# Late attention in two parts: products with v by row halves, one output product behind the scores

## The chip, the cores and the metric

The kernel runs on one core of a Trainium2 chip. The metric is the time of one execution on the device in microseconds (us). Short names: PE is the matmul engine (TensorE), PEld its loads of stationary operands, DVE is VectorE, ACT is ScalarE, POOL is GpSimd, SP the engine that issues most DMA transfers. Matmuls write into PSUM banks of 512 fp32 per partition; everything else lies in SBUF.

## The reference, cut to what matters

Attention over chunks of 32 queries (16 keys to the left, 8 to the right, and 8 memory keys: 64 keys a chunk), then a gated feed-forward on the rows of all heads:

```
for c in range(nc):                                  # 24 chunks of 32, per batch and head
    k_full = np.concatenate([mem_k, k_ctx], axis=2)  # 64 keys, some left out at the ends
    scores = scale * np.matmul(q_c, k_full.transpose(0, 1, 3, 2))
    scores = scores - np.max(scores, axis=-1, keepdims=True)
    a = np.exp(scores)
    a = a / (np.sum(a, axis=-1, keepdims=True) + 1e-09)
    out[:, :, c_start:c_end] = np.matmul(a, v_full)
...
rms = np.sqrt(np.mean(x * x, axis=-1, keepdims=True) + 1e-06)
xn = x / rms * rms_g
g = xn @ w_gate
silu = g * (1.0 / (1.0 + np.exp(-g)))
return (silu * (xn @ w_val) @ w_out)                 # 3072 x 512, w: 512 x 1536 and 1536 x 512
```

## The kernel before

**Feed-forward.** The 3072 rows are 8 blocks of 384 tokens, and the 1536 columns of the weights are 12 groups `f` of 128. For each block and `f`, `moe_in` makes the gate `pg` and the value `pv` (12 matmuls of 384 columns each), DVE and ACT make `t`, and split it into `hh` and `hl`, and `moe_out` adds 9 matmuls of 512 columns into three banks `po` (an output product). All of it runs in fp32r with operands split into a high and a low part. `moe_out` of group f-1 stands behind `pv` of group f, so that `hh` and `hl` have one group of matmuls as cover.

**Attention.** It is cut into 32 units: a batch, a half of its 768 queries, and a pair of heads. Units 0 to 7 (blocks 0 and 1) are done at the start, by an order that is written out by hand, together with the making of the split weights. The other 24 are "late": twelve pairs of units, done while the feed-forward runs. The feed-forward is then a row of seven segments: the rest of block 0 (from f = 5), and blocks 2 to 7. While one segment runs, the attention of the next block (two pairs of units) is done, and its rows are normed.

**A late visit.** `late_steps` is a generator, and one step of it is called a visit. `VISITS` says at which places of a segment the visits stand: place 2(f-f0) is behind `pg` of group f, place 2(f-f0)+1 behind `pv`. A visit has work for the pair before (`old`) and for the current pair (`cur`), in this order on PE:

- `stage_p`: six 128x128 transposes of the old pair's probabilities `pe` into two banks `pT` (the first is the bank of `pg`, tag "g");
- `stage_c`, on ACT and DVE: `pT` is copied into the buffers `pt0` and `qp1`, in four copies of 64 partitions x 384, two on each engine. The even and the odd chunk of a pair of chunks go to columns of their own, and what is left between them is zero (the buffers were set to zero once by POOL), so that one stationary operand of 128 rows holds the keys of both chunks;
- `stage_s2`: 48 score matmuls of the current pair, on tiles of 64 rows x 32 columns of the array, 64 columns each;
- `stage_m`, `stage_e` on DVE and ACT: maximum, difference, exponential;
- `stage_o`: the products with v of the old pair, 12 matmuls a unit, 128 rows x 64 columns of the array, 64 columns each, in two banks (the second is the bank of `pv`, tag "v");
- `late_r`: ACT copies each unit's result to `xT` and squares it, DVE adds the squares; after a block's second pair `late_n` makes the norm in steps ("n" in `VISITS`): two matmuls `ssum`, a polynomial for the inverse root on DVE, and at last `xT` times the norm;
- `stage_d` on DVE: sums and division of the current pair's exponentials; then the loads of q and k for the next pair and of v for the current one, on SP's queue, into single buffers.

At the end of a segment `split_x` splits `xT` into `xh` and `xl` on ACT and DVE for the next segment, with the last `hh` and `hl` between.

An fp32 matmul of these shapes stands as two instructions in the trace. The order in which PE runs what is written is fixed from the late part on (`keep_in_program_order`); on DVE, ACT and SP a scheduler places instructions by priority and estimated times, except where `issue_after` binds them.

Of the kernel before, what the change touches and what calls it, by code (L numbers as in the profile page):

```python
# [20 lines left out]
CH = 32  # L21
# [18 lines left out]
YMAX = 0x1DFE / 0x1000 * 2.0 ** -96  # L40


VISITS = (((1, "v"), (5, "v"), (9, "v"), (10, "n"), (11, "n"), (12, "n")),
# [3 lines left out]
RSQRT = (-0.49999831, 0.37499999, -0.31395044, 0.27418771)  # L47
FA, FC = 1, 5
SEQ = ([(0, f) for f in range(FA)] + [(1, f) for f in range(FA)] + [(b, f) for f in range(FA, FC) for b in range(2)]
# [21 lines left out]
def tile_kernel(ctx: ExitStack, tc: tile.TileContext, q, k, v, w_gate, w_val, w_out, rms_g, out):  # L71
# [46 lines left out]
    pts = [early.tile([P, NT, 4, 2, CH], F32, name=f"pt{i}") for i in range(2)]  # L118
    late = {}

    def zeros(t):
        nc.gpsimd.memset(t, 0.0)
        return t

    def late_buffers(i):

        if i:
            t = p1.tile([P, HT + VN], F32, name="qp1", tag="A")
            late["q", 1], late["pt", 1] = t[:, 0:HT], zeros(t[:, HT:])
            late["kv", 1] = p1.tile([P, KN + VN], F32, name="kv1", tag="B")  # L130
        else:
            late["q", 0] = p1.tile([P, HT], F32, name="q0", tag="q")
            late["pt", 0] = zeros(p1.tile([P, VN], F32, name="pt0", tag="wy"))
            late["kv", 0] = p1.tile([P, KN + VN], F32, name="kv0", tag="ws")
        late["pt", i] = late["pt", i].rearrange("p (i a s q) -> p i a s q", i=NT, a=4, s=2)

    def load_qk(u):
        d = st.setdefault(u, {})
# [16 lines left out]

    def pt_of(u):

        return pts[u % 2] if u < NE else late["pt", u % 2]

    def copy(e, out, in_):  # L160
        if e == "a":
# [68 lines left out]
    def stage_d(u):  # L230
        stage_da(u)
        stage_db(u)
# [31 lines left out]
        d["t"] = t  # L264

    def stage_c(u):
        stage_ch(u, 0, "a")
        stage_ch(u, 1, "d")

    def stage_ch(u, hh, e):  # L270
        r = slice(64 * hh, 64 * hh + 64)
        t4 = st[u]["t"][:, 0:HT].rearrange("p (i a q) -> p i a q", i=NT, q=CH)
        copy(e, pt_of(u)[r, :, :, hh, :], t4[r])

    def stage_o(u, tag=None):

        pt, vw = pt_of(u), st[u]["v"]
        o = psum_m(tag, f"o{u}") if tag else psum_a(f"o{u}")
        for j in range(NJ):
            for hh in range(2):  # L280
                on_pe(nc.tensor.matmul(o[64 * hh:64 * hh + 64, j * D:(j + 1) * D], lhsT=vw[:, j, hh],  # L281
                                 rhs=pt[:, j // 2, 2 * (j % 2) + (hh ^ (u % 2 if u >= NE else 0))].rearrange("p c q -> p (c q)"),
                                 start=True, stop=True))
        st[u]["o"] = o[:, 0:HT]

    def late_r(u, x):

        g = units[u][2]
        o = st.pop(u)["o"]
        nc.scalar.copy(x[:, g], o)  # L290
        s = obuf(f"sq{u}")[:, 0:HT]
        nc.scalar.activation(s, x[:, g], AF.Square)
        if g:
            nc.vector.tensor_tensor(out=s, in0=s, in1=late["ss"], op=ALU.add)
        late["ss"] = s

    def late_n(x):

        ss = late["ss"]
        sh, sl = [p3.tile([P, DM], F32R, name=f"s{c}", tag="stg")[:, 0:HT] for c in "hl"]  # L300
        nc.scalar.copy(sh, ss)
        nc.vector.tensor_tensor(out=sl, in0=ss, in1=sh.bitcast(F32), op=ALU.subtract)
        yield
        ps = psum_a("ssum")[:, 0:HT]
        for i, c in enumerate((sh, sl)):
            on_pe(nc.tensor.matmul(ps, lhsT=one.broadcast_to([P, P]), rhs=c, start=not i, stop=i == 1))
        s = obuf("rs")[:, 0:HT]
        nc.vector.tensor_scalar(out=s, in0=ps, scalar1=DM * 1e-6, scalar2=None, op0=ALU.add)

        r = obuf("rr")[:, 0:HT]  # L310
        nc.scalar.activation(r.bitcast(I32), s.bitcast(U32), AF.Copy, bias=float(0x5F3759DF), scale=-0.5)
        t = obuf("rt")[:, 0:HT]
        nc.vector.tensor_tensor(out=t, in0=r, in1=r, op=ALU.mult)
        nc.vector.tensor_tensor(out=t, in0=t, in1=s, op=ALU.mult)
        nc.vector.tensor_scalar(out=t, in0=t, scalar1=1.0, scalar2=None, op0=ALU.subtract)
        yield
        q = obuf("rq")[:, 0:HT]
        nc.vector.tensor_scalar(out=q, in0=t, scalar1=RSQRT[3], scalar2=RSQRT[2], op0=ALU.mult, op1=ALU.add)
        nc.vector.tensor_tensor(out=q, in0=q, in1=t, op=ALU.mult)
        for c in (RSQRT[1], RSQRT[0]):  # L320
            nc.vector.scalar_tensor_tensor(out=q, in0=q, scalar=c, in1=t, op0=ALU.add, op1=ALU.mult)
        nc.vector.scalar_tensor_tensor(out=r, in0=q, scalar=1.0, in1=r, op0=ALU.add, op1=ALU.mult)
        yield
        for kt in range(NKT):
            nc.vector.scalar_tensor_tensor(out=x[:, kt], in0=x[:, kt], scalar=rg[:, kt:kt + 1], in1=r,  # L325
                                           op0=ALU.mult, op1=ALU.mult)
        yield
# [162 lines left out]
    def obuf(name):  # L490
        return p3.tile([P, DM], F32, name=name, tag="stg")
# [64 lines left out]
    def late_steps():  # L556


        pairs = [(u, u + 1) for u in range(NE, len(units), 2)]
        for n in range(len(pairs) + 1):  # L560
            old = pairs[n - 1] if n else ()
            cur = pairs[n] if n < len(pairs) else ()
            new = pairs[n + 1] if n + 1 < len(pairs) else ()
            for u in old[0:1]:
                if u % NG == 0:
                    late_x["x"] = p1.tile([P, NKT, HT], F32, name="xT", tag="x")
            x = late_x.get("x")
            with tc.high_priority():
                for i, u in enumerate(old):
                    stage_p(u, None if i else "g")  # L570
                for u in old:
                    stage_c(u)
            if not cur:
                yield "p"
            with tc.high_priority():
                if cur:
                    stage_s2(cur)
                for u in cur:
                    stage_m(u)
                for u in cur:  # L580
                    stage_e(u)
                for i, u in enumerate(old):
                    stage_o(u, "v" if cur and i else None)
                for u in old:
                    late_r(u, x)
            norm = late_n(x) if n and n % 2 == 0 else ()
            if norm:
                with tc.high_priority():
                    next(norm)
            with tc.high_priority():  # L590
                for i, u in enumerate(cur):
                    if norm and i:
                        with tc.issue_after(last_of(nc.vector)):
                            stage_d(u)
                    else:
                        stage_d(u)
            for u in new:
                load_qk(u)
            for u in cur if n else ():
                load_v(u)  # L600
            yield "v"
            for _ in norm:
                yield "n"

# [148 lines left out]
    for sg, (blk, f0) in enumerate(segments):  # L753
        po = [psm_o(i) for i in range(NT)] if sg else sp["po", 0]
        last = sg == len(segments) - 1
        steps = {} if last else dict(VISITS[min(sg, 2) + (sg == len(segments) - 2)])

        def visit(gap):
            if gap in steps and next(todo, None) not in (steps[gap], None):
                raise AssertionError(gap)  # L760
        for f in range(f0, NF):
            g = moe_in("g", f, xs, last)
            visit(2 * (f - f0))
            out_ = lambda f=f, h=prev: moe_out(f - 1, h, po)
            if f == f0:
                out_ = lambda: None
                if sg == 0:

                    moe_out(NF - 1, prev, po1)
                    with tc.high_priority():  # L770
                        store(1, po1)
            vv = moe_in("v", f, xs, last)
            visit(2 * (f - f0) + 1)
            if f < NF - 1:
                out_()
                prev = moe_h(g, vv, blk)
            elif last:
                out_()
                finish(f, g, vv, po, blk)
            else:  # L780
                with tc.high_priority():
                    t = moe_t(g, vv, blk)
                xs = split_x(late_x["x"], t, out_, lambda h: moe_out(NF - 1, h, po))
        if sg == 0:
            behind.close()
        if not last:
            store(blk, po)
# [65 lines left out]
```

## Time and profile before

| | before |
|---|---|
| runs, median (lowest to highest) | 709.34 us (708.74 to 709.37) |
| the profiled execution, own time | 707.74 us |
| its span, first to last instruction | 705.9 us |
| mean granted TensorE clock | 0.992 |
| DVE busy | 392.3 us (56%) |
| ACT busy | 261.4 us (37%) |
| HBM read, written | 47.97 MB, 6.29 MB |

The profiled execution is one of its own beside the three timed runs; its time contains 1.84 us outside its span. In the views, a line has a start, a duration in us, the engine, the source line, the operation, what it writes and reads, shapes, and a count. A matmul's duration runs from its start until its last result, and matmuls overlap: the cost of one is read from the distance between starts.

### The profile page before, as it was taken

What the parts mean: (1) busy time and instruction counts of PE and PEld (TensorE: products, weight loads), DVE (VectorE), ACT (ScalarE), POOL (GpSimd) and SP (SyncE); (2) the same over time, 40 slices, a digit from 0 to 9 for tenths busy, and PEclk for the clock granted to TensorE, in tenths of its full rate; (3) what the DMA queues carried; (4) which work ended last, traced back from release to release, by engine and by line L of the source; (5) the groups of instructions that cost most, each with busy time, mean ns of one, the idle gap of its engine ahead of it and who ended that gap; (6) DMA issues with size and microseconds to landing.
All of it is one profiled execution on the core that took longest, in us unless ns stands there. A gap on an engine that the chain in (4) does not pass through costs nothing.

```text
span 705.9 us, 13419 instructions
## 1 busy us (share of the span) xinstructions
PE 687.4 (97%) x5702; PEld 636.3 (90%) x5702; DVE 392.3 (56%) x780; ACT 261.4 (37%) x474; POOL 6.1 (1%) x14
## 2 busy tenths in 40 slices
PE   7899999999999999999999999999999999999997
PEld 6798898999989999999999999999999999999996
DVE  6789999857674327552383525735276532552222
ACT  4697987733333113331233313222133311331112
POOL 0010000000000000000000000000000000000000
PEclk8899999999999999999999999999999999999999
DMA  9644644333321103130021303013031100010001
GB/s 319 246 167 137 235 149 139 115 132 109 115 90 51 58 0 105 46 104 1 17 90 45 105 1 89 16 46 105 1 104 46 45 3 0 1 46 1 0 1 46
DMA packets 22620, 55.14 MB, mean 78 GB/s; under 512 B 2464, under 2 KB 6816, under 8 KB 22560
## 3 DMA queue, kind: packets, MB, share of 16 engines
q1 hardware_dynamic: 19824, 49.55, 20.9%
q10 hardware_dynamic: 2736, 4.72, 1.8%
q8 instruction: 45, 0.74, 0.5%
q14 instruction: 15, 0.12, 0.1%
HBM read 47.97 MB, written 6.29 MB: 77 GB/s over the span
## 4 chain that ended last, share of the span: by engine, by line
PE 88%; DVE 5%; ACT 4%; issue 1%; DMA 1%; POOL 0%; SPq 0%; DVEq 0%; ACTq 0%
PE pg L437 27%; PE pv L437 27%; PE po L487 27%; PE o L281 3%; PE pT L263 1%; ACT pt L162 1%; DVE pt L165 1%; DVE qp L165 1%; DMA k<-in_k_dram 1%; ACT ws L392 1%; ACT ws L381 1%; PE s L184 1%; PE ss L622 1%; ACT wy L382 1%; DVE xT L325 1%
## 5 line engine op out<-in xcount | busy, mean ns | idle before, releaser
L437 PE MATMUL pv<-xh,wh_v 128*128 128x384 f32 x384 | 130.1, 339 | 2.1 <-DVE t L458 2.1
L437 PE MATMUL pg<-xh,wh_g 128*128 128x384 f32 x384 | 130.5, 340 | 0.0
L437 PE MATMUL pv<-xh,wl_v 128*128 128x384 f32 x384 | 129.7, 338 | 0.5 <-DVE wl_v L408 0.5
L437 PE MATMUL pg<-xl,wh_g 128*128 128x384 f32 x384 | 129.8, 338 | 0.0
L437 PE MATMUL pg<-xh,wl_g 128*128 128x384 f32 x384 | 129.8, 338 | 0.0
L437 PE MATMUL pv<-xl,wh_v 128*128 128x384 f32 x384 | 129.6, 337 | 0.0
L162 ACT CAST hh<-t 128x384 fp32r<-128x384 f32 x89 | 45.8, 515 | 192.7 <-PE po L487 176.0
L487 PE MATMUL po<-wh_o,hh 128*128 128x512 f32 x285 | 113.9, 400 | 0.7 <-ACT hh L744 0.6
L487 PE MATMUL po<-wh_o,hl 128*128 128x512 f32 x285 | 112.6, 395 | 0.0
L487 PE MATMUL po<-wl_o,hh 128*128 128x512 f32 x285 | 112.3, 394 | 0.0
L455 DVE SCALAR_TENSOR_TENSOR t<-t,pg 128x384 f32<-128x384 f32 x72 | 39.9, 554 | 105.8 <-ACT t L451 105.7
L467 DVE TENSOR_TENSOR hl<-t,hh 128x384 fp32r<-128x384 f32 x89 | 49.5, 556 | 85.7 <-ACT hh L162 85.6
L458 DVE TENSOR_TENSOR t<-t,pv 128x384 f32<-128x384 f32 x95 | 52.7, 554 | 71.5 <-PE pv L437 70.2
L451 ACT ACTIVATE t<-pg 128x384 f32<-128x384 f32 x72 | 35.5, 493 | 120.2 <-PE pg L437 120.2
L437 PEld LDWEIGHTS pg<-xh,wh_g 128*128 128x128 f32 x384 | 72.3, 188 | 4.1 <-DVE gr L446 0.4
L437 PEld LDWEIGHTS pg<-xl,wh_g 128*128 128x128 f32 x384 | 72.3, 188 | 3.6
L437 PEld LDWEIGHTS pv<-xh,wh_v 128*128 128x128 f32 x384 | 72.0, 188 | 3.6 <-DVE t L458 1.8
L437 PEld LDWEIGHTS pv<-xh,wl_v 128*128 128x128 f32 x384 | 72.0, 188 | 0.8 <-DVE wl_v L408 0.8
L437 PEld LDWEIGHTS pg<-xh,wl_g 128*128 128x128 f32 x384 | 72.2, 188 | 0.0
L437 PEld LDWEIGHTS pv<-xl,wh_v 128*128 128x128 f32 x384 | 72.1, 188 | 0.1
L487 PEld LDWEIGHTS po<-wh_o,hl 128*128 128x128 f32 x285 | 53.6, 188 | 13.6 <-DVE hl L745 0.6
L487 PEld LDWEIGHTS po<-wh_o,hh 128*128 128x128 f32 x285 | 53.5, 188 | 10.7 <-ACT hh L744 1.6
(110 smaller groups left out, 717.2 us busy)
## 6 DMA issues: line engine op xcount, KB each, us to landing
kv<-in_v_dram SPq DMA_DIRECT2D x24, 384.0 KB, 5.6
kv<-in_k_dram SPq DMA_DIRECT2D x24, 312.0 KB, 4.2
out_dram<-ob ACTq DMA_DIRECT2D x18, 256.0 KB, 2.1
ws<-in_moe_w_gate_dram SPq DMA_DIRECT2D x4, 1024.0 KB, 4.9
ws<-in_moe_w_val_dram SPq DMA_DIRECT2D x4, 1024.0 KB, 5.0
ws<-in_moe_w_out_dram SPq DMA_DIRECT2D x4, 1024.0 KB, 5.0
q<-in_q_dram SPq DMA_DIRECT2D x20, 192.0 KB, 3.1
vw<-in_v_dram SPq DMA_DIRECT2D x8, 384.0 KB, 7.3
```

Of the source, the lines that this page charges most:

```text
L162: return nc.scalar.copy(out, in_)
L165: return nc.vector.tensor_copy(out=out, in_=in_)
L184: nc.tensor.matmul(s[a:a + CH, o:o + KC], lhsT=d["q"][r, c * CH:c * CH + CH], rhs=k[r], start=True, stop=True)
L263: on_pe(nc.tensor.transpose(out=t[:, i * P:(i + 1) * P], in_=pe[:, i * P:(i + 1) * P], identity=ident))
L281: on_pe(nc.tensor.matmul(o[64 * hh:64 * hh + 64, j * D:(j + 1) * D], lhsT=vw[:, j, hh], rhs=pt[:, j // 2, 2 * (j % 2) + (hh ^ (u % 2 if u ...
L325: nc.vector.scalar_tensor_tensor(out=x[:, kt], in0=x[:, kt], scalar=rg[:, kt:kt + 1], in1=r, op0=ALU.mult, op1=ALU.mult)
L437: on_pe(nc.tensor.matmul(ps[:, 0:HT], lhsT=weight(a, n, f, kt), rhs=xs[c][:, kt], start=kt == 0 and i == 0, stop=kt == NKT - 1 and i == 2))
L451: nc.scalar.activation(t, g, AF.Tanh, scale=0.5)
L455: nc.vector.scalar_tensor_tensor(out=t, in0=t, scalar=1.0, in1=g, op0=ALU.add, op1=ALU.mult)
L458: nc.vector.tensor_tensor(out=t, in0=t, in1=vv, op=ALU.mult)
L467: nc.vector.tensor_tensor(out=hl, in0=t, in1=hh.bitcast(F32), op=ALU.subtract)
L487: on_pe(nc.tensor.matmul(po[i], lhsT=h[a][:, i * P:(i + 1) * P], rhs=weight(c, "o", f), start=f == 0 and n == 0, stop=f == NF - 1 and n == 2))
```

## The change

Each visit is split in two. Part "s": transposes, copies, scores, and what DVE and ACT make of them, and the loads of q and k for the next pair. Part "o", behind the output product that follows place x (called place x.5): products with v, `late_r`, `stage_d`, loads of v. The last pair's transposes and products stood apart before, at places 17 and 18 of the last segment but one; now they are at 17 and 17.5 as in the others.

The products with v are written by row halves: the even chunk's 64 keys stand in rows 0 to 63 and the odd chunk's in rows 64 to 127, each with 32 columns of its own, so `pT` is copied as it stands, one copy of 128 x 384 a unit (ACT for the even unit, DVE for the odd one), without zeros between. Instead of 24 matmuls a pair (128 rows x 64, 64 columns) there are 48 (64 rows x 64, 32 columns), and the row halves write to two banks, `oe` and `oo`, each with both units in it. `late_r` reads each bank once.

In the first late segment the third visit goes from place 9 to 7, and the norm's steps from 10, 11, 12 to 9, 10, 11. In the last segment with visits the norm's steps go from 20, 21, 22 to 19, 20, 21.

```diff
-VISITS = (((1, "v"), (5, "v"), (9, "v"), (10, "n"), (11, "n"), (12, "n")),
-          ((5, "v"), (17, "v"), (19, "n"), (20, "n"), (21, "n")),
-          ((5, "v"), (17, "v"), (19, "n"), (20, "n"), (21, "n")),
-          ((5, "v"), (17, "p"), (18, "v"), (20, "n"), (21, "n"), (22, "n")))
+VISITS = (((1, "s"), (5, "s"), (5.5, "o"), (7, "s"), (7.5, "o"), (9, "n"), (10, "n"), (11, "n")),
+          ((5, "s"), (5.5, "o"), (17, "s"), (17.5, "o"), (19, "n"), (20, "n"), (21, "n")))
...
     def stage_c(u):
-        stage_ch(u, 0, "a")
-        stage_ch(u, 1, "d")
+        copy("da"[u % 2 == 0], late["pt", u % 2], st[u]["t"][:, 0:HT])
...
+    def stage_o2(pair, tag):
+        st["o2"] = o2 = [psum_a(f"oe{pair[0]}"), psum_m(tag, f"oo{pair[0]}") if tag else psum_a(f"oo{pair[0]}")]
+        for j in range(NJ):
+            for n, u in enumerate(pair):
+                pt = late["pt", u % 2].rearrange("p (j e q) -> p j e q", j=NJ, e=2)
+                for cp in range(2):
+                    r, o = slice(64 * cp, 64 * cp + 64), (NJ * n + j) * CH
+                    for hh in range(2):
+                        on_pe(nc.tensor.matmul(o2[cp][64 * hh:64 * hh + 64, o:o + CH], lhsT=st[u]["v"][r, j, hh],
+                                               rhs=pt[r, j, hh ^ u % 2], start=True, stop=True))
...
+        xc = x[:, g:g + 2].rearrange("p g (j c q) -> p g j c q", c=2, q=CH)
+        for cp in range(2):
+            nc.scalar.copy(xc[:, :, :, cp], o2[cp][:, 0:HT].rearrange("p (g j q) -> p g j q", g=2, q=CH))
...
-                for i, u in enumerate(old):
-                    stage_o(u, "v" if cur and i else None)
-                for u in old:
-                    late_r(u, x)
+            for u in new:
+                load_qk(u)
+            if old:
+                yield "s"
+                with tc.high_priority():
+                    stage_o2(old, "v")
+                    late_r(old, x)
...
             visit(2 * (f - f0) + 1)
             if f < NF - 1:
                 out_()
+                visit(2 * (f - f0) + 1.5)
                 prev = moe_h(g, vv, blk)
```

On PE, at the second visit (first late segment, place 5), the scores `s10` and `s11` are followed by the products `o8` and `o9` before; `po` is the output product:

```order
L200 MATMUL s10_1960<-kv0_1718,q0_1715 32x64 x2
L200 MATMUL s11_1961<-kv1_1742,qp1_1740 32x64 x2
L281 MATMUL o8_2020<-pt0_1716,kv0_1718 64x64 x12
L281 MATMUL o9_2033<-qp1_1740,kv1_1742 64x64 x12
L487 MATMUL po0_808<-wh_o3_1082,hh_1917 128x512
L487 MATMUL po0_808<-wl_o3_1083,hh_1917 128x512
```

and now the same place, from the end of the scores on:

```order
L193 MATMUL s11_1957<-kv1_1740,qp1_1739 32x64 x2
L496 MATMUL po0_808<-wh_o3_1082,hh_1915 128x512
L496 MATMUL po0_808<-wl_o3_1083,hh_1915 128x512
L496 MATMUL po0_808<-wh_o3_1082,hl_1917 128x512
L496 MATMUL po1_809<-wh_o3_1082,hh_1915 128x512
L496 MATMUL po1_809<-wl_o3_1083,hh_1915 128x512
L496 MATMUL po1_809<-wh_o3_1082,hl_1917 128x512
L496 MATMUL po2_810<-wh_o3_1082,hh_1915 128x512
L496 MATMUL po2_810<-wl_o3_1083,hh_1915 128x512
L496 MATMUL po2_810<-wh_o3_1082,hl_1917 128x512
L287 MATMUL oe8_2029<-pt0_1716,kv0_1717 64x32 x2
L287 MATMUL oo8_2030<-pt0_1716,kv0_1717 64x32 x2
```

The nine `po` matmuls moved between the scores and the products, and the products go to `oe` and `oo` in turn.

On DVE, at the third visit (`pe12` and `pe13` are the current pair, `sq` the squares, `sl` the low part of their sum, which `ssum` reads), this stood before:

```order
L223 TENSOR_TENSOR pe13_2229<-s13_2174,mx13_2227 128x384
L246 MEMSET pe12_2225 64x8
L250 TENSOR_REDUCE r12_2271<-pe12_2225 128x6
L294 TENSOR_TENSOR sq10_2260<-sq10_2260,sq9_2050 128x384
L251 TENSOR_SCALAR r12_2271<-r12_2271 128x6
L252 RECIPROCAL r12_2271<-r12_2271 128x6
L256 TENSOR_TENSOR pe12_2225<-pe12_2225,r12_2271 128x384
L246 MEMSET pe13_2229 64x8
L294 TENSOR_TENSOR sq11_2264<-sq11_2264,sq10_2260 128x384
L250 TENSOR_REDUCE r13_2277<-pe13_2229 128x6
L467 TENSOR_TENSOR hl_2306<-t_2300,hh_2304 128x384
```

and this stands there now:

```order
L216 TENSOR_TENSOR pe13_2202<-s13_2147,mx13_2200 128x384
L476 TENSOR_TENSOR hl_2303<-t_2297,hh_2301 128x384
L303 TENSOR_TENSOR sq2_2271<-sq2_2271,sq1_2083 128x384
L303 TENSOR_TENSOR sq3_2274<-sq3_2274,sq2_2271 128x384
L311 TENSOR_TENSOR sl_2278<-sq3_2274,sh_2277 128x384
L239 MEMSET pe12_2198 64x8
L239 MEMSET pe13_2202 64x8
L455 TENSOR_TENSOR gr_2351<-pg_2305,rb0_149 128x384
L243 TENSOR_REDUCE r12_2281<-pe12_2198 128x6
L243 TENSOR_REDUCE r13_2287<-pe13_2202 128x6
```

The squares' sums, which wait for the products with v, now stand ahead of the division of both units and of the next group's `gr`; all of that waits behind them.

More of the change, by code (lines that the diff above doesn't have):

```diff
@@ L119, in tile_kernel @@
     late = {}
-    def zeros(t):
-        nc.gpsimd.memset(t, 0.0)
-        return t
     def late_buffers(i):
         if i:
-            t = p1.tile([P, HT + VN], F32, name="qp1", tag="A")
-            late["q", 1], late["pt", 1] = t[:, 0:HT], zeros(t[:, HT:])
+            t = p1.tile([P, 2 * HT], F32, name="qp1", tag="A")
+            late["q", 1], late["pt", 1] = t[:, 0:HT], t[:, HT:]
             late["kv", 1] = p1.tile([P, KN + VN], F32, name="kv1", tag="B")
@@ L132, in late_buffers @@
             late["q", 0] = p1.tile([P, HT], F32, name="q0", tag="q")
-            late["pt", 0] = zeros(p1.tile([P, VN], F32, name="pt0", tag="wy"))
+            late["pt", 0] = p1.tile([P, HT], F32, name="pt0", tag="wy")
             late["kv", 0] = p1.tile([P, KN + VN], F32, name="kv0", tag="ws")
-        late["pt", i] = late["pt", i].rearrange("p (i a s q) -> p i a s q", i=NT, a=4, s=2)
     def load_qk(u):
@@ L156, in pt_of @@
     def pt_of(u):
-        return pts[u % 2] if u < NE else late["pt", u % 2]
+        return pts[u % 2]
     def copy(e, out, in_):
@@ L281, in stage_o, with late_r @@
                 on_pe(nc.tensor.matmul(o[64 * hh:64 * hh + 64, j * D:(j + 1) * D], lhsT=vw[:, j, hh],
-                                 rhs=pt[:, j // 2, 2 * (j % 2) + (hh ^ (u % 2 if u >= NE else 0))].rearrange("p c q -> p (c q)"),
+                                 rhs=pt[:, j // 2, 2 * (j % 2) + hh].rearrange("p c q -> p (c q)"),
                                  start=True, stop=True))
         st[u]["o"] = o[:, 0:HT]
[L286 to L295, printed above, removed]
+    def stage_o2(pair, tag):
[8 more added lines that the diff above has]
+                                               rhs=pt[r, j, hh ^ u % 2], start=True, stop=True))
+    def late_r(pair, x):
+        g = units[pair[0]][2]
+        o2 = st["o2"]
+        for u in pair:
+            st.pop(u)
+        xc = x[:, g:g + 2].rearrange("p g (j c q) -> p g j c q", c=2, q=CH)
+        for cp in range(2):
+            nc.scalar.copy(xc[:, :, :, cp], o2[cp][:, 0:HT].rearrange("p (g j q) -> p g j q", g=2, q=CH))
+        for i in range(g, g + 2):
+            s = obuf(f"sq{i}")[:, 0:HT]
+            nc.scalar.activation(s, x[:, i], AF.Square)
+            if i:
+                nc.vector.tensor_tensor(out=s, in0=s, in1=late["ss"], op=ALU.add)
+            late["ss"] = s
     def late_n(x):
@@ L572, in late_steps @@
                     stage_c(u)
-            if not cur:
-                yield "p"
-            with tc.high_priority():
                 if cur:
@@ L581, in late_steps @@
                     stage_e(u)
-                for i, u in enumerate(old):
-                    stage_o(u, "v" if cur and i else None)
-                for u in old:
-                    late_r(u, x)
+            for u in new:
[5 more added lines that the diff above has]
+                    late_r(old, x)
             norm = late_n(x) if n and n % 2 == 0 else ()
+            behind = ExitStack()
             if norm:
@@ L589, in late_steps @@
                     next(norm)
[L590 to L598, printed above, removed]
+                behind.enter_context(tc.issue_after(last_of(nc.vector)))
+            with tc.high_priority(), behind:
+                for u in cur:
+                    stage_d(u)
             for u in cur if n else ():
                 load_v(u)
-            yield "v"
+            yield "o" if old else "s"
             for _ in norm:
@@ L755, in tile_kernel @@
         last = sg == len(segments) - 1
-        steps = {} if last else dict(VISITS[min(sg, 2) + (sg == len(segments) - 2)])
+        steps = {} if last else dict(VISITS[min(sg, 1)])
         def visit(gap):
```

## The prediction

> **What bounds the kernel now.** I read the page's busy shares first, then PE's order of time at one visit after another, then what PE waits for, and last the ends of the segments. The page's first line:
>
> ```profile
> PE 687.4 (97%) x5702; PEld 636.3 (90%) x5702; DVE 392.3 (56%) x780; ACT 261.4 (37%) x474; POOL 6.1 (1%) x14
> ```
>
> PE is the bound, so only what shortens PE's own row of work, or closes a hole in it, can count. The third visit, in order of time on PE (start, duration):
>
> ```profile
> 186.63 0.82 PE L263 MATMUL pT<-ident,pe 128*128 128x128 f32 x6
> ...
> 187.38 0.25 PE L200 MATMUL s<-kv,q 64*32 64x64 f32 x2
> ...
> 188.32 0.23 PE L200 MATMUL s<-kv,qp 64*32 64x64 f32 x2
> 188.75 0.92 PE L281 MATMUL o<-pt,kv 128*64 128x64 f32 x24 [0.20 <-DVE qp L165]
> 189.50 0.87 PE L281 MATMUL o<-qp,kv 128*64 128x64 f32 x24
> 190.30 0.50 PE L487 MATMUL po<-wh_o,hh 128*128 128x512 f32 x1
> 190.64 0.40 PE L487 MATMUL po<-wl_o,hh 128*128 128x512 f32 x1
> 190.87 0.40 PE L487 MATMUL po<-wh_o,hl 128*128 128x512 f32 x1
> ```
>
> Starts count, not durations. Two po starts are 0.23 us apart when nothing disturbs (190.64 to 190.87). So the visit costs PE 190.64 - 0.23 - 186.63 = 3.78 us. Eleven visits have all parts (from the second to the twelfth); the second, read in the same way from 170.12 us on, costs 0.05 more, the other ten agree with this one to about 0.01. Within the visit, products start at 188.75 although the last score started at 188.32: they wait for the second copy on DVE, here with the first operation behind it:
>
> ```profile
> 188.14 0.55 DVE L165 COPY qp<-pT 64x384 f32<-64x384 f32 x1
> 188.73 1.02 DVE L211 TENSOR_REDUCE mx<-s 128x6 f32<-128x384 f32 x2
> ```
>
> The copy ends at 188.69. PE's view of waits sums what it saw of this:
>
> ```profile
> PE o L281 <- DVE qp L165: 2.3, 11, 0.3
> ```
>
> 2.3 us in 11 waits, the longest 0.3. That is small, and not all of it comes back when the wait goes.
>
> **The visit after the change.** What scores cost without a wait behind them is seen at the very first visit, which has scores alone:
>
> ```profile
> 158.35 0.25 PE L200 MATMUL s<-kv,q 64*32 64x64 f32 x2
> ...
> 159.45 0.44 PE L437 MATMUL pg<-xh,wh_g 128*128 128x384 f32 x1
> 159.73 0.34 PE L437 MATMUL pg<-xl,wh_g 128*128 128x384 f32 x1
> ```
>
> From the first score to pg 1.10 us, and pg's first step is 0.28 where 0.175 is usual (2.11 us for 12): a restart costs 0.11. In the visit above, scores to products took 188.75 - 187.38 = 1.37 (the scores start there; their 0.75 behind pT). What products cost between two projections stands at the last visit, where they are behind pg already:
>
> ```profile
> 604.13 0.34 PE L437 MATMUL pg<-xh,wl_g 128*128 128x384 f32 x1
> 604.40 0.92 PE L281 MATMUL o<-pt,kv 128*64 128x64 f32 x24
> 605.15 0.87 PE L281 MATMUL o<-qp,kv 128*64 128x64 f32 x24
> 605.95 0.44 PE L437 MATMUL pv<-xh,wh_v 128*128 128x384 f32 x1
> ```
>
> Into the products 0.27 - 0.175 = 0.09 lost, the products themselves 1.55, and 0.11 again in the restart of pv. So, with X for the new products, a visit will cost 0.75 (pT) + 1.10 (scores) + 0.11 (restart of po) + 0.09 (into the products) + X + 0.11 (restart of pg) = 2.16 + X. Splitting the visit costs one more switch; taking the wait away gives 1.37 - 1.10 = 0.27, and 0.20 of it goes back for the switch. The Trainium skill, page "TensorEngine Tiling (Array Packing)", section "Key Properties", says that a change of the tiling mode drains the array; by it the four changes of shape per visit, where three were, would make the split lose time. The trace agrees that each costs about 0.1, and the sum has them.
>
> **X, the new products.** Per pair 96 instructions (48 written, two each) instead of 48, on tiles half as tall, with half the moving columns. Rows that tell what paces small tiles:
>
> ```profile
> 33.84 0.90 PE L184 MATMUL s<-k,q 64*32 64x64 f32 x48
> 34.66 0.92 PE L281 MATMUL o<-pt,vw 128*64 128x64 f32 x24
> ```
>
> ```profile
> 39.88 1.26 PE L173 MATMUL warm<-zero 128*64 128x64 f32 x18
> 41.08 0.87 PE L263 MATMUL pT<-ident,pe 128*128 128x128 f32 x6
> 41.79 1.40 PE L622 MATMUL ss<-onef,xq 128*128 128x1 f32 x12
> ```
>
> "warm" stays on one tile of 64 array columns: (1.26 - 0.22 of the last one's duration) / 17 = 0.061, and 0.058 behind the first step. "ss" has one moving column and 128 array columns, and takes about 0.11 a step, as pT does with 128 moving columns. So a step on a tile goes with the array columns whose operand is loaded, not with the moving columns: 128 take 0.11, 64 take 0.058. The scores' 32 fit: 48 instructions in 0.90 - 0.22, on two tiles at a time, are 0.029 a step and tile. Half the moving columns therefore buy nothing. The old products keep two tiles busy (the two 64-column halves): 48 / 2 x 0.058 = 1.39, and 0.16 for start and end make the 1.55 seen. The new ones have four tiles: 96 / 4 x 0.058 = 1.39, the same. X is between these bounds: 1.11 if they run at the pace of the late scores (96 in 0.95, 188.32 against 187.38, so 0.0099 a start, plus 0.16), and 2.94 if only two tiles run at a time, as in the old products (96 / 2 x 0.058 + 0.16). I take 1.55: the shape of the load is that of "warm" and the old products, and the late scores show that more than two tiles run at once (two at a time would take them 48 x 0.029 = 1.39, not 0.95).
>
> Visits: ten save 3.78 - 3.71 = 0.07, the second 0.12: 0.8 us together. The first visit (scores alone) and the last one's products stay as they are.
>
> **The moved places.** In the first late segment the norm's ssum waits for sl, the low part of the sum of squares:
>
> ```profile
> 194.62 0.33 PE L306 MATMUL ssum<-sh,one 128*128 128x384 f32 x1
> 195.09 0.44 PE L306 MATMUL ssum<-sl,one 128*128 128x384 f32 x1
> 195.37 0.34 PE L437 MATMUL pv<-xh,wh_v 128*128 128x384 f32 x1
> ```
>
> 0.75 instead of two steps of 0.175: 0.40 lost. And at the segment's end the last output product waits for hh:
>
> ```profile
> 205.66 0.40 PE L487 MATMUL po<-wh_o,hl 128*128 128x512 f32 x1
> 206.68 0.50 PE L487 MATMUL po<-wh_o,hh 128*128 128x512 f32 x1 [0.62 <-ACT hh L744]
> 207.02 0.40 PE L487 MATMUL po<-wl_o,hh 128*128 128x512 f32 x1
> 207.28 0.50 PE L487 MATMUL po<-wh_o,hl 128*128 128x512 f32 x1
> ```
>
> ```profile
> 204.48 1.15 DVE L325 SCALAR_TENSOR_TENSOR xT<-xT,rg,rr 128x384 f32<-128x384 f32 x2
> 205.53 0.55 DVE L458 TENSOR_TENSOR t<-t,pv 128x384 f32<-128x384 f32 x1
> ```
>
> The step 205.66 to 206.68 has 0.79 too much, and the three behind it 0.10, 0.03 and (by the same pattern) 0.10: 1.0 us. The cause stands in the second fence: t of the last group is queued on DVE behind xT times the norm. The norm's steps come one place earlier, which is one projection and one output product (4.2 us), the third visit two places earlier. Laid out with the before-trace's durations (a DVE operation of 384 columns every 0.47, of the norm's chain 0.58), sl is ready about 0.8 us ahead of the ssum that reads it, xT is done before gr of the last group, and hl comes about 0.2 us late at the last product. So 0.4 comes back, and 0.8 of the 1.0; I give the remainder from 0 to 0.6, since this stretch keeps DVE without a pause. The last segment with visits ends in the same way:
>
> ```profile
> 623.01 0.40 PE L487 MATMUL po<-wh_o,hl 128*128 128x512 f32 x1
> 623.50 0.50 PE L487 MATMUL po<-wh_o,hh 128*128 128x512 f32 x1
> ```
>
> 0.49 for 0.23, and the same restart behind it: 0.25 + 0.23 = 0.5, which goes to nothing, since no current pair loads DVE there and the norm has one place more.
>
> **What I cost at nothing, and its cover.** The copies now have the scores (1.1) and nine po (2.1) as cover; they are also one per engine and not two. ACT reads oe and oo into xT in 0.5 each, and pv of the next group, which overwrites oo's bank, comes one projection (2.1) behind the products, where an output product and a projection (4.2) stood before: cover left 1.1. ssum at places 19 has 4.2 behind the products, where 6.3 stood; copies, two squares, two sums, sh and sl take about 3.7: 0.5 left. The zeroing on POOL goes; nobody waited for it. SP's queue: in the first late segment the gap between second and third visit falls from 16.5 to 10 us, and q, k and v are reloaded into single buffers in it:
>
> ```profile
> kv<-in_v_dram SPq DMA_DIRECT2D x24, 384.0 KB, 5.6
> kv<-in_k_dram SPq DMA_DIRECT2D x24, 312.0 KB, 4.2
> ```
>
> The loads of k go out when the scores end (about 172) and are needed at 181; those of v when the products end (176), landing at about 182, needed at 184.3. 2 us are left. DVE finishes the division for the third visit's transposes at about 177.6, needed at 180.1.
>
> **Sum.** 0.8 + 0.4 + 0.8 + 0.5 = 2.5 us less. Against the profiled execution's own time of 707.74 (span 705.9) that is 705.2; the median of the runs lies 1.6 above that execution, and on that base it is 709.34 - 2.5 = 706.8 us. 0.2%, or 1.4 us, is about what a measurement of this kernel tells from no change.
>
> **Rivals.**
> - *The products run no faster than two at a time.* One mechanism, at twelve places: starts stay 0.029 apart, X = 2.94, and 12 x 1.39 = 16.7 us are added: 723.5. It decides from X = 1.55 + 2.5 / 12 = 1.76 on, above which the change loses. For it: the only rows with 64-column loads have two tiles; against it: the late scores. The Trainium skill, page "TensorE: Matmul & The Clock Gate", section "Wait — 56ns, not 53.3ns?", gives a floor of about 25 ns between starts however few the columns; by it alone X would be an estimated 2.56 us and the time about 719. The late scores' 0.0099 between starts on different tiles disagrees, so I give it little.
> - *They run four at a time, but with the scores' losses.* 96 / 4 x 0.029 would be 0.70 for the late scores, which take 0.95. The same 0.25 lost per pair gives X = 1.80, 3.0 more: 709.8, no change that can be told. For it: same engine, same number of instructions; against it: the slower step leaves the engine twice the time to feed the tiles.
> - *Shorter tiles load faster.* X = 1.11, 5.3 less: 701.5. For it: no row has 64 rows with 64 columns; against it: 0.029, 0.058, 0.11 follow the columns exactly.
> - *The saved waits come back elsewhere* (sl, hl, or v late in the crowded first segment): the moved places give nothing, 709.34 - 0.8 = 708.5.
>
> **How the numbers follow.** Forecast as summed 0.62 (705.4 to 708.0 alone); faster loads 0.14; the scores' losses 0.11; two at a time, or anything with X above 1.9, 0.08; waits come back 0.05. Faster: 0.60 + 0.14 + 0.01 = 0.75; same: 0.02 + 0.08 + 0.04 = 0.14; slower: 0.03 + 0.08 = 0.11. The range is 702.0 to 709.6: it holds the forecast, half of the faster loads, most of the scores' losses and the waits that come back, and leaves out the two-at-a-time case.
>
> **What would show it.** In the trace after: eleven waits of PE for qp gone; scores to po 1.10 and 0.11; products as 96 instructions in about 1.55 from first start to pg, with four starts per 0.058; ssum 0.35 at all six places; no step above 0.4 in the last po of the first late segment. I am wrong if the products take above 1.7 or below 1.4 a pair, or if PE shows a new wait at the third visit, at ssum or at pv behind the products.

## The result, and the profile after

704.42 us (median of 4, 703.95 to 705.35) against 709.04 (median of 4, 707.66 to 709.37: the three runs of the table before and a fourth): ratio 0.994, interval 0.9922 to 0.9958. Of all the runs told of here one is left out as disturbed, a fourth of the kernel with two tiles at a time (733.24 us, granted clock 0.971 against 0.983 to 0.988 in the other three). The profiled execution of the change took 704.78 with a span of 703.0, where 707.74 and 705.9 stood. The page's first line, which answers to the one shown of before:

```profile
PE 688.0 (98%) x6278; PEld 636.4 (91%) x6278; DVE 383.9 (55%) x768; ACT 257.6 (37%) x462; POOL 4.7 (1%) x12
```

PE has 576 matmul instructions more, 12 x 48, for 0.6 us more of busy time. The third visit in order of time on PE (start, duration):

```profile
180.53 0.81 PE L256 MATMUL pT<-ident,pe 128*128 128x128 f32 x6
181.28 0.25 PE L193 MATMUL s<-kv,q 64*32 64x64 f32 x2
...
182.38 0.50 PE L496 MATMUL po<-wh_o,hh 128*128 128x512 f32 x1
182.72 0.40 PE L496 MATMUL po<-wl_o,hh 128*128 128x512 f32 x1
...
184.36 0.40 PE L496 MATMUL po<-wh_o,hl 128*128 128x512 f32 x1
184.68 0.25 PE L287 MATMUL oe<-pt,kv 64*64 64x32 f32 x2
184.70 0.25 PE L287 MATMUL oo<-pt,kv 64*64 64x32 f32 x2
...
186.22 0.45 PE L446 MATMUL pg<-xh,wh_g 128*128 128x384 f32 x1
186.50 0.34 PE L446 MATMUL pg<-xl,wh_g 128*128 128x384 f32 x1
```

From pT to scores 0.75, from scores to po 182.38 - 181.28 = 1.10, po's restart 0.34 - 0.23 = 0.11, into the products 0.32 - 0.23 = 0.09, the products 1.53, pg's restart 0.28 - 0.175 = 0.11: 3.69 in all, for 3.78. The other visits agree with this one. Four starts come together (two oe, two oo, one for each tile), and 24 such groups make the 1.53. The two ends that the moved places were to mend, first the sum for the norm, then the last output product of the first late segment:

```profile
190.55 0.34 PE L315 MATMUL ssum<-sh,one 128*128 128x384 f32 x1
190.73 0.34 PE L315 MATMUL ssum<-sl,one 128*128 128x384 f32 x1
190.90 0.39 PE L496 MATMUL po<-wh_o,hh 128*128 128x512 f32 x1
...
205.38 0.40 PE L496 MATMUL po<-wh_o,hl 128*128 128x512 f32 x1
205.68 0.50 PE L496 MATMUL po<-wh_o,hh 128*128 128x512 f32 x1
...
206.60 0.40 PE L496 MATMUL po<-wh_o,hh 128*128 128x512 f32 x1
```

Two usual steps of 0.175 for ssum; at the end 206.60 - 205.38 = 1.22 for four steps, 0.3 more than 4 x 0.23, where 1.0 stood. The end of the last segment with visits has no step over 0.24 now. Summed over all steps of PE from the first late scores on that are longer than usual, the visits give 1.1 us, ssum 0.4, the two ends 0.7 and 0.5: 2.7. PE's whole late row, from the first late score to the start of the last matmul, took 539.57 us where 542.87 stood, which is 3.3 less; the other 0.6 is spread over some 2500 steps of usual length, and nothing here says why.

### The profile page after: what moved, and what is told of

Read it like the earlier page. It is cut to its first block, busy times and chain, and to the rows that moved or that the text cites. A ratio compares the mean times of both kernels' runs of the same rounds, so it can differ in the third digit from the quotient of the medians.

```text
span 703.0 us, 14521 instructions
## 1 busy us (share of the span) xinstructions
PE 688.0 (98%) x6278; PEld 636.4 (91%) x6278; DVE 383.9 (55%) x768; ACT 257.6 (37%) x462; POOL 4.7 (1%) x12
## 4 chain that ended last, share of the span: by engine, by line
PE 94%; DVE 3%; ACT 2%; issue 1%; POOL 0%; DVEq 0%; ACTq 0%; POOLq 0%
PE pg L446 28%; PE pv L446 28%; PE po L496 27%; PE oe L287 2%; PE s L193 2%; PE pT L256 2%; PE warm L166 1%; PE ss L627 1%; PE o L273 1%; ACT ws L401 1%; PE s L177 1%; PE oo L287 1%; ACT ws L390 0%; PE po L524 0%; PE ssum L315 0%
```

## The experiments

Each was timed beside the kernel before on the same chip; ratios are to that.

**The change, timed again.** 

> The changed kernel itself, timed again. PE's steps in the two traces differ by 2.7 us in all (visits 1.0, sum for the norm 0.4, end of the first late segment 0.7, end of the last segment with visits 0.5), but the medians differ by 4.6 (709.04 to 704.42, interval of the ratio 0.9922 to 0.9958). Theory A: the steps are the whole gain, the rest is scatter of four runs: 2.4 to 3.4 us faster than before. Rival B: something that the late part's steps don't show (the early part, or all steps a little faster) gives 1.5 more: 4.0 to 5.0 us faster.

705.26 against 708.39, ratio 0.9951 (0.9938 to 0.9964), 2.6 to 4.4 us. Theory A's 2.7 lies within, though near its end. The whole late row fits better: it took 539.63 us in this second trace, 3.2 less than before. PE's first late scores start between 156.7 and 160.1 us in the eleven profiles taken here, whatever the kernel, so the part ahead of the change scatters by more than is looked for. Much of that is the clock: three stretches of 3.41 us at half the granted clock lie ahead of the first late score in seven profiles (156.7 to 158.7), four in the other four (158.9 to 160.1).

**Split and products at the old places.**

```
-(7, "s"), (7.5, "o"), (9, "n"), (10, "n"), (11, "n")
+(9, "s"), (9.5, "o"), (11, "n"), (11.5, "n"), (12, "n")   # last segment with visits: n at 20, 21, 22
```

> The split and the new products stay; the third visit of the first late segment goes back to place 9 (products at 9.5, norm's steps at 11, 11.5 and 12), the last segment's norm back to 20 to 22. Theory A: the two segment ends come back (0.7 + 0.5), visits stay at 3.69 and the sum's 0.4 stays gained, since it still has an output product and a projection behind the products: 1.2 us slower than the changed kernel, a step of about 0.8 over the usual one in the last output product of the first late segment. Rival: the moved places carry most of the gain (3 us slower), or none (the ends were only covered by the split: no slower).

707.05, ratio 0.9982 (0.9968 to 0.9996): about 2 us slower than the changed kernel, not 1.2. Visits are at 3.69 and ssum at 0.35, as expected. The end of the first late segment is worse than it was before the change:

```profile
204.70 0.40 PE L497 MATMUL po<-wh_o,hl 128*128 128x512 f32 x1
205.87 0.50 PE L497 MATMUL po<-wh_o,hh 128*128 128x512 f32 x1 [0.77 <-ACT hh L750]
...
208.28 0.34 PE L447 MATMUL pg<-xh,wh_g 128*128 128x384 f32 x1
209.16 0.45 PE L447 MATMUL pg<-xl,wh_g 128*128 128x384 f32 x1 [0.54 <-DVE xl L747]
```

0.93 at the first wait, and 0.7 at a second, since products half a place later push the norm, and with it the splitting of xT, into the next segment's first projection. So with the split visit the earlier place is worth more than the wait that was seen before. Without it the split and the new products leave little: PE's long steps sum to 0.1 us less than in the kernel before, the whole late row is 0.6 shorter, and the run is 0.3 to 2.3 faster.

**The moved places alone.** In the kernel before:

```
-(9, "v"), (10, "n"), (11, "n"), (12, "n")                  +(7, "v"), (9, "n"), (10, "n"), (11, "n")
-(17, "p"), (18, "v"), (20, "n"), (21, "n"), (22, "n")      +(16, "p"), (17, "v"), (19, "n"), (20, "n"), (21, "n")
```

> The kernel before with its old visits and old products, but the third visit at place 7 with the norm at 9 to 11, and in the last segment with visits transposes at 16, the rest at 17, the norm at 19 to 21. Theory A: 1.6 us faster than before (0.4 for the sum, 0.7 and 0.5 for the segment ends), visits at 3.78; the gains of the split and of the places add up to the whole. Rival: without the split the crowded first late segment gives the 0.7 back as a wait for loads or for the division: 0.9 faster or less.

707.27, ratio 0.9981 (0.997 to 0.9992): 0.6 to 2.1 us faster. The rival's crowding isn't there, the first late segment ends without a wait. But my edit for the last segment made a wait of its own: the transposes at place 16 want the bank of pg before its reader is done.

```profile
595.43 0.33 PE L437 MATMUL pg<-xh,wl_g 128*128 128x384 f32 x1
596.93 0.87 PE L263 MATMUL pT<-ident,pe 128*128 128x128 f32 x6 [1.17 <-DVE t L455]
```

1.3 us are lost there of the expected 1.6; PE's steps sum to 0.5 less than before. So the run shows that the moves pay without the split, and not how much they pay together.

**Transposes alone, scores and products together.**

```
                 for u in old:
                     stage_c(u)
+            if old:
+                yield "p"
...
                     stage_m(u)
+                if old:
+                    stage_o2(old, "v")
+                    late_r(old, x)
```

with the letter p at the places 5, 7 and 17. 

> Another cut of the same visit: transposes alone at the first place, scores and products together behind the output product. The transposes have the shape of a projection, and at the last visit, where an output product follows them, they cost 0.66 in all, where 0.75 stand before scores; and scores run into products without a projection between them. Theory A: a visit costs 0.57 + 0.08 + 0.10 + (1.0 to 1.1) + 1.53 + 0.11 = 3.4 to 3.5 instead of 3.69: 11 visits save 2 to 3 us against the changed kernel. Rival: scores into products cost the same 0.2 as a restart, or the scores half a place later make the third visit's transposes wait for the division: no gain, or up to 1 us slower.

715.57, ratio 1.0108 (1.0071 to 1.0146), 7 us slower. The visit's arithmetic held: at a visit without a stop,

```profile
267.75 0.82 PE L256 MATMUL pT<-ident,pe 128*128 128x128 f32 x6
268.32 0.48 PE L496 MATMUL po<-wh_o,hh 128*128 128x512 f32 x1
...
270.27 0.40 PE L496 MATMUL po<-wh_o,hl 128*128 128x512 f32 x1
270.60 0.25 PE L193 MATMUL s<-kv,q 64*32 64x64 f32 x2
...
271.70 0.25 PE L287 MATMUL oe<-pt,kv 64*64 64x32 f32 x2
...
273.23 0.44 PE L446 MATMUL pg<-xh,wh_g 128*128 128x384 f32 x1
```

0.57 + 0.08 + 0.10 + 1.10 + 1.53 + 0.11 = 3.49. But five of eleven visits have a hole in the products, which nothing in the profile ends ("issue"); one of them, and PE's view of waits:

```profile
227.59 0.22 PE L287 MATMUL oo<-pt,kv 64*64 64x32 f32 x1
229.48 0.24 PE L287 MATMUL oo<-pt,kv 64*64 64x32 f32 x1 [1.68 <-issue]
```

```profile
PE oo L287 <- issue: 4.6, 3, 1.7
PE oe L287 <- issue: 2.6, 2, 1.5
```

From start to start the five are 1.3 to 1.9 us, 8.3 together. The rest is ssum at 0.73 at three places (the norm's chain is behind the softmax there) and a half clock behind this stop: the stretch with the stop and the one behind it, busy time and instructions of PE, PEld, DVE, ACT and POOL, then PEclk, DMA share and GB/s:

```profile
226.00:229.60 3.60, 1.93 (x148) 1.72 (x127) 3.11 (x7) 1.06 (x3) 0.00 (x0) 1.00 0.39 79
230.20:233.40 3.20, 3.20 (x16) 3.13 (x12) 2.11 (x7) 1.80 (x4) 0.00 (x0) 0.50 0.99 347
```

The granted clock was 0.50 in the whole second stretch, and a step of pg took 0.32 instead of 0.175. The Trainium skill, page "TensorE: Matmul & The Clock Gate", section "Part 1: The HAM clock gate (the "warmup" mystery)", ties the half clock to an idle window of about 3.4 us. A stop of 1.9 us was enough to bring it here; the stops of 1.81 and 1.73 us in the same trace brought none (more on this in the next run).

The five stops have one thing in common. Count all of PE's recorded instructions from the start (matmuls, weight loads and the few for semaphores): the number that stands ahead of a stop is 193 modulo 256 each time. A row of scores and new products has 385, so it holds one or two such boundaries, and the page shows loads of that size: 49 on the instruction queue for 2 x 6278 matmuls and weight loads, 256 for each (packets, MB, share of the DMA engines' span):

```profile
q8 instruction: 49, 0.80, 0.5%
```

**New products right behind the scores.** Is it the regrouping, or the length of the row?

```
             if old:
-                yield "s"
                 with tc.high_priority():
                     stage_o2(old, "v")
```

> The changed kernel with the new products back right behind the scores, no output product between (everything of a visit at places 5, 7 and 17). In the regrouped kernel PE stopped for 1.3 to 1.9 us in the middle of five of eleven rows of scores and products, each time when 193 matmuls and weight loads of a group of 256 had been recorded, with a load on the instruction queue near by. Theory A (instructions run out): a row of scores and new products, 2 x 192 recorded instructions, is too dense for the loads of instructions, so stops of 1 to 2 us stand here too in some four to six visits, and besides the wait for the copy is back (visit 3.75 in the others): 6 to 12 us slower than the changed kernel. Rival B (the stops belong to the regrouped order alone, by the loads of q and k that start in the middle): no stops, 0.07 x 11 = 0.8 us slower than the changed kernel.

719.0, ratio 1.0154 (1.0129 to 1.0179), 14 us slower than the changed kernel, more than theory A's 12. Seven visits stop for 0.55 to 2.05 us, all seven at 193 modulo 256 again, four are followed by a half clock. So it is not the regrouping. (The last visit, which has no scores to cover the copies, waits 0.2 us ahead of its products and has a hole of 0.3 among them.) PE's waits put seven holes on "issue", 4.9 and 3.5 us together.

Why some stops cost clock and others don't shows in the times. The half clocks last 3.41 us each and begin on one grid of that step. In the stretch of the grid just ahead of a half clock PE was busy for 1.74 us in the regrouped run and for 1.58, 1.73, 2.00 and 2.05 us here. The least busy late stretch that no half clock followed had 2.13 us, in the run that comes next. The stops of 1.81 and 1.73 us fell across two stretches and left PE at least 2.36 us in each. So for these stops it counts how much of one falls into a single stretch; the half clocks of the two-tile run further down came without a stop.

One part of A was wrong: the wait for the copy isn't back. Scores to products take 1.10 at all eleven visits. With one copy per unit and engine instead of two the copy is ready under the scores alone.

**The boundary moved.** The regrouped kernel with 54 instead of 22 warm-up matmuls at the start, so that all later instructions stand 128 further on. 

> The regrouped kernel with the new products (the one that stops), and nothing changed but the warm-up at the very start: 54 matmuls there instead of 22. Each is recorded as 4 instructions on PE (two matmuls, two weight loads), so all that follows stands 128 instructions later. In both kernels that stop, every stop over 0.5 us lies where the count of PE's recorded instructions is 192 or 193 modulo 256, at the second such boundary within one row of scores and products; rows with only one boundary never stop. Theory A (blocks of 256 instructions that are loaded too late): with the shift the boundaries lie elsewhere in the rows. The five visits that stopped (third, fourth, ninth, tenth, eleventh counted from the one with scores alone) run clean; the sixth, seventh and eighth, which were clean, hold two boundaries now, the second at 371, 344 and 313 instructions into the row (the visits near 312, 354 and 396 us), and stop for 1 to 2 us there; the next (near 437 us, second boundary at 286) may stop briefly or not. Rival B (the q and k loads, or the visit itself): the same five visits stop as before.

711.15, ratio 1.0058 (1.0026 to 1.0089). The three visits that were named by their times stop, and no other (the five that stopped before are the third, fourth and the tenth to twelfth; the expectation's ordinals for the last three are one too low). The rows of the two kernels, with the places in the row (of 385) at which a count of 193 modulo 256 falls:

| visit | regrouped: boundaries in the row | stop, us | shifted: boundaries | stop, us |
|---|---|---|---|---|
| 2 | 29, 285 | none | 157 | none |
| 3 | 76, 332 | 1.53 | 204 | none |
| 4 | 45, 301 | 1.89 | 173 | none |
| 5 | 18, 274 | none | 146 | none |
| 6 | 243 | none | 115, 371 | 1.37 |
| 7 | 216 | none | 88, 344 | 1.49 |
| 8 | 185 | none | 57, 313 | 1.38 |
| 9 | 158 | none | 30, 286 | none |
| 10 | 127, 383 | 1.81 | 255 | none |
| 11 | 100, 356 | 1.30 | 228 | none |
| 12 | 69, 325 | 1.73 | 197 | none |

```profile
312.97 0.22 PE L287 MATMUL oe<-qp,kv 64*64 64x32 f32 x1
314.34 0.24 PE L287 MATMUL oe<-qp,kv 64*64 64x32 f32 x2 [1.15 <-issue]
```

Neither the q and k loads nor the code of the visit moved. So PE's instructions come in blocks of 256, and a stop stands at the second boundary in a dense row. Not at every one: boundaries at 274, 285 and 286 went free here, while 261 and 292 of the unsplit kernel stopped for 0.77 and 0.55.

What decides is not the place in the row but the time of the load. The traces have the start and end of each load on the instruction queue. At the fifteen stops of the three kernels the load for the second boundary went out near PE's passing of the first (0.7 to 1.5 us behind it; 0.2 behind and 0.3 ahead at 261 and 292) and took 0.9 to 1.5 us, and PE went on 1.25 to 1.56 us behind its end. From the load's start that is 2.2 to 2.8 us, while PE ran the 256 instructions between two boundaries of a free row in 1.65. At 274, 285 and 286 the load had gone out 1.4 to 1.6 us ahead of the first boundary. Over all 513 boundaries in the eleven traces that have a load to go with them (in order: the first load with the second boundary, and so on), PE passed none sooner than 1.23 us behind that load's end. What sends a load out earlier or later isn't shown.

The kernel before has such a stop too, in its early part:

```profile
24.17 0.49 PE L622 MATMUL ss<-onef,xq 128*128 128x1 f32 x3
26.80 1.06 PE L622 MATMUL ss<-onef,xq 128*128 128x1 f32 x9 [2.13 <-issue]
```

The count ahead of it is 961, again 193 modulo 256, and the load ended at 25.35, 1.45 us before PE went on. Ten of the eleven profiles have this stop (0.6 to 2.4 us from start to start); the shifted kernel, whose boundaries lie elsewhere, has two others in the early scores instead (2.2 and 1.8 us).

The Trainium skill, page "Runtime: NRT & Kernel Launch", section "Instruction fetch mechanics", gives the blocks of 256 too, and calls a crossing mostly hidden; in rows of small matmuls (256 instructions in 1.65 us) the stops show that it isn't. The changed kernel's rows have 192 instructions, hold at most one boundary, and show no gap above 0.06.

**The old products behind the output product.** In the changed kernel stage_c, stage_o, late_r and the buffers are those of before (128 rows, zeros, one bank for each unit):

```
-                    stage_o2(old, "v")
-                    late_r(old, x)
+                    for i, u in enumerate(old):
+                        stage_o(u, "v" if i else None)
+                    for u in old:
+                        late_r(u, x)
```

> The changed kernel with the old products of 128 rows (48 instructions a pair, two copies with zeros beside, one bank per unit) behind the output product; same places. Theory A: products cost the same on PE either way (1.55 against 1.53), and the two copies have 3.2 us of cover: 0 to 0.4 us slower than the changed kernel; the row halves and two banks buy next to nothing, the place behind the output product is the gain of a visit. Rival: the new products carry the visits' gain: 1 us slower.

704.74, ratio 0.994 (0.9928 to 0.9953): the whole gain. Products take 1.548 against 1.532, and no visit waits. The row halves and the two banks buy nothing that can be measured.

**Two tiles at a time.**

```
-        for j in range(NJ):
-            for n, u in enumerate(pair):
+        for cp in range(2):
+            for j in range(NJ):
+                for n, u in enumerate(pair):
```

> The changed kernel with the loop over row halves outermost in the products: the same 48 written matmuls a pair, but first all of the upper row half, so that only two tiles take turns. Theory A: a step on a tile takes 0.058 whatever moves, so two at a time take 96 / 2 x 0.058 + 0.16 = 2.94 a pair instead of 1.53: 12 x 1.41 = 16.9 us slower than the changed kernel. Rival: starts are limited by the engine's supply, not by the tile (about 14.5 ns a start whatever the tile): no slower.

722.57 (median of three, 720.99 to 724.87), ratio 1.0185 (1.0164 to 1.0206), 17 us slower than the changed kernel. The products of a pair:

```profile
187.13 0.30 PE L287 MATMUL oe<-pt,kv 64*64 64x32 f32 x4
...
189.63 0.28 PE L287 MATMUL oo<-qp,kv 64*64 64x32 f32 x4
189.85 0.45 PE L446 MATMUL pg<-xh,wh_g 128*128 128x384 f32 x1
```

2.72 instead of 1.53, expected 2.94: the tile, not the supply, sets the pace. Two steps on each of two tiles take 0.1167 us in the trace, and one step on each of four tiles takes 0.0583 in the changed kernel, so a step on a tile is 0.058 either way, as the expectation had it. The 2.72 is less than 2.94 since in the middle of the row, where the upper half ends and the lower begins, some 16 starts go to four tiles after all. 12 x 1.19 are 14.2; PE's steps in the profiled run (724.87) add 18.6 in all, and the other 4.4 are put down to three half-clock stretches, each behind such a pair (3 of 12). PE was busy throughout, ahead of them too; the one shown (columns as above):

```profile
490.30:493.50 3.20, 3.20 (x11) 3.20 (x11) 0.56 (x1) 0.93 (x3) 0.00 (x0) 0.50 0.75 209
```

**Regrouped, with the old products.** The rows have 288 instructions; at visits ahead of the norm products come first, then scores:

```
+                for part in "os" if n % 2 == 0 else "so":
+                    if part == "s" and cur:
+                        stage_s2(cur)
...
+                    if part == "o" and old:
+                        for i, u in enumerate(old):
+                            stage_o(u, "v" if i else None)
```

> The regrouped visit (transposes alone, then an output product, then scores and products in one row) with the old products of 48 instructions, and at the visits ahead of the norm products first, scores behind. A row then has 288 recorded instructions instead of 384, as in the kernel before, which showed no stop there. Theory A: no stops, or at most a short one; visits at 3.49 to 3.50 instead of 3.69, the norm's sum at 0.35: 1.5 to 2.2 us faster than the changed kernel, if the third visit's transposes don't wait for the division; with products first there they may wait up to 1.5 us once. Rival: 288 in a row without a wait between also run out of instructions: stops of 0.5 to 1.5 us at a few visits, no faster than the changed kernel.

701.56 (700.65 to 702.51), ratio 0.99 (0.9886 to 0.9915), which lies below both intervals of the change: it beats both kernels. No stop stands in any late row, ssum is 0.35 everywhere, and a visit costs 3.51:

```profile
261.35 0.82 PE L261 MATMUL pT<-ident,pe 128*128 128x128 f32 x6
261.92 0.48 PE L485 MATMUL po<-wh_o,hh 128*128 128x512 f32 x1
...
264.21 0.92 PE L279 MATMUL o<-pt,kv 128*64 128x64 f32 x24
...
266.85 0.44 PE L435 MATMUL pg<-xh,wh_g 128*128 128x384 f32 x1
```

The third visit's transposes wait 0.1 for the division, not 1.5. PE's steps sum to 2.05 less than in the changed kernel. That the rows went free is not proof that 288 instructions are safe: only two of them hold a second boundary (at 285 and 256), and both loads had gone out 1.5 us or more ahead of the first.

## Why the prediction was right

- **Direction, range and size.** 706.8 was forecast, 704.42 measured, and 705.26 the second time. The long steps gave 2.7 where the sum said 2.5. As a gain, 2.5 was somewhat too small: 4.6 and 3.1 were measured, and PE's late row is 3.3 shorter. The range of 702.0 to 709.6 is wide enough to hold the time of the kernel before, so that the time lies in it says little; the terms below say more.
- **X** was 1.53, forecast 1.55. The row-based price of a load of 64 columns held, and "half the moving columns buy nothing" too: the old products take 1.548 at the same place.
- **Visits**: 1.1 instead of 0.8, since a visit takes 3.69, not 3.71. **ssum**: 0.40, as summed. **First late segment's end**: 0.73 of 1.0, forecast 0.8, with the remainder of 0.3 inside the 0 to 0.6 that was given. **Last segment with visits**: 0.49, forecast 0.5.
- **Rivals.** Two tiles at a time doesn't happen in the changed order; forced, it takes 2.72 and the time is 722.57, near the 723.5 worked out. That it came so near is partly luck, since a quarter of the loss on PE came from the clock and not from the tiles. The rule of the Trainium skill, page "TensorE: Matmul & The Clock Gate", section "Wait — 56ns, not 53.3ns?", of some 25 ns between starts doesn't hold where four tiles take turns: 1.53 / 96 = 16 ns, start and end of the row included. Nothing pointed to faster loads or to the scores' losses.
- **What failed in the reasoning**, without moving the number. "Taking the wait away gives 0.27, and 0.20 of it goes back for the switch" put the gain on the split. The unsplit run has no wait either: one copy per engine removes it alone, and the split costs 0.2 a visit. What the split is needed for was missing from the list of things costed at nothing: 48 more matmuls and their weight loads a pair, right behind the scores, run into the block loads of PE's instructions. Their cover is the output product between, and that cover gone costs 14 us. With the old products, which give the same time in the changed order, that danger wasn't seen.
- **Still open**: why some 2500 ordinary steps took 0.6 us less in all, and what of the first timing's 4.6 lies beyond the 3.3 of PE's late row. The ratio's interval, 3.0 to 5.5 us, takes in the 3.3.

## What to carry to other kernels

Price small matmuls by the tile: the number of loads, their columns, and how many tiles take turns; the moving columns and the split into row halves didn't matter here. Count the instructions in any dense row as well, matmuls and weight loads: here 385 in a row cost up to 2 us where two block boundaries fell into them, and 288 showed no stop, with two such rows among them, so put a stretch of large matmuls between such rows, or write the row with fewer instructions. Transposes, which fill the array as a projection does, cost no switch between projections; scores and products next to each other pay for one instead of two.

## What was new on the hardware

- PE's instructions arrive 256 at a time, and a stop of mostly 1.3 to 2.05 us stands at the second boundary in a row of 385 small ones, unless its load went out early; 128 more instructions ahead moved the stops to exactly the visits worked out.
- PE passes a boundary no sooner than 1.23 us behind the end of the load that goes with it (513 boundaries); the fifteen late stops end 1.25 to 1.56 us behind it.
- The granted clock fell to 0.50 for 3.41 us behind five of the seven stops of 1.6 to 2.05 us, and three times in twelve behind 2.7 us of products on two tiles, with PE never idle.
- A step on one 64x64 tile took 0.058 us with two tiles in turn and with four, so that four tiles make twice the steps in the same time.
